# Both chunks of an attention unit in one run of narrow matmuls, and a fixed table for the order of all instructions

## The chip, the cores and the metric

The kernel runs on one core of one Trainium2 chip. The metric is the time of the device for one execution, in microseconds (us). TensorE (PE) does matmuls, VectorE (DVE) and ScalarE (ACT) work on tiles, GpSimd (POOL) only sets constants here, and SyncE (SP) issues every transfer.

## What is computed

Gated linear attention with a complex decay per key row, and then a two-layer feed-forward network on its output:

```python
for t in range(S):                       # S = 768, B = 4, H = 8, D = 48
    new_re = ar * S_re - ai * S_im       # ar, ai: normalised gate of step t, per key row
    new_im = ar * S_im + ai * S_re
    kv = np.einsum('bhd,bhe->bhde', k[:, :, t], v[:, :, t])
    S_re, S_im = (new_re + kv, new_im)
    y[:, :, t] = np.einsum('bhd,bhde->bhe', q[:, :, t], S_re)
...
h = x @ w_in                             # x: 3072 x 384, w_in: 384 x 2048
g = np.where(h >= 1, h, np.where(h <= -1, 0.0, (h + 1) ** 2 / 4))
return g @ w_out                         # 2048 x 384
```

## The kernel before, in words

The 3072 tokens are cut into 12 units of 256 tokens (`u`), and a unit into two chunks of 128 (`c`). Units alternate between two batch entries; a unit is the first, second or third part (`PART`) of its sequence of 768. Two units make a block of 512 tokens, six blocks in all.

**Gates.** `gates(u)` turns a and the inputs k and q into rotated, decayed rows with long ACT and DVE instructions over 768 or 1536 columns; the last two (`turn`, L958) write products that ten DMAs (`spread`) move into the tiles `hd`, one set of rows per head.

**Attention.** `attend(u)` works per chunk in five steps. `scores` makes the masked products of k and q (`sc`, L1129; DVE masks them into `am`, L1137). `transposes` turns k (`tp`, L1072; ACT copies into `kT`). `values` makes the output `yp` from the state `st` (L1170) and from `am` and V (L1178); ACT copies it to `xr` (L1190). `products` makes k times V (`dp`, L1101), and DVE adds it to the state (`st`, L1114; the first chunk of a sequence is copied by ACT, L1111). `values` and `products` use half of the array's columns (their weights are 64 columns wide, "128*64" in a row); all other matmuls use 128. A unit is issued in five visits of PE: `sc` of chunk 0; `tp` of chunk 0; `yp` and `dp` of chunk 0 with half of `sc` of chunk 1; the other half with `tp` of chunk 1; `yp` and `dp` of chunk 1. So a unit has two narrow runs, with wide work between them. The results of `sc`, `tp`, `dp` and `yp` take turns in three PSUM banks.

**Handing over.** A block's x needs 16 rows of two heads moved to other partitions. For blocks 1 to 5 six small DMAs per unit do it (`move`); for block 0 PE does it with a selecting matrix (`joined`, `px`, L1262), twelve matmuls for each of its two units. `split` then makes xH and xL.

**Network.** `moe(blk)` runs 16 steps (`f`): nine matmuls `h` (L1351), on ACT and DVE a chain from `s` (L1376) over `g` (L1395, L1403) and `gh` (L1409) to `gl` (L1413), then nine matmuls `o` (L1426). In blocks 0 and 1 ACT has two more instructions in the chain (L1386, L1390) and DVE one less. `s` and `g` take turns in three tiles, `gh` and `gl` in six, `h` in two PSUM banks. The three results of a block are copied by ACT (L1453) and stored. The weights come as raw bits and are decoded by DVE and ACT during the head and block 0 (L546 to L575); for the first five of sixteen the low part is made by PE (`rest`, L584, L585, `LO_PE`).

**Order.** All of this is written down as operations with costs and dependencies; `Plan.forward` plays them through by due times and gives the order that each engine's queue gets. `Plan.order` starts from due times worked out backwards and tries 1000 changes of them. SP's queue carries all DMAs in the planned order. Until the first `h`, PE is kept busy with matmuls whose result is not used (`idle`, L1481).

Of the kernel before, what the change touches and what calls it, by code (L numbers as in the profile page):

```python
# [45 lines left out]
LATER = 4  # L46
SUM = 1.0e6
RATIO = 1.5
FOURTH = 1.142**4
# [14 lines left out]
LOAD, MOVE = 410.0, 240.0  # L64
LATE = 2000
LATE_MOVE = 1000
# [3 lines left out]
LAG = 3  # L70
# [14 lines left out]
LO_PE = 5  # L85
INFLATE = 1.6
SPLIT_DUE = 3000
TO_NARROW, TO_WIDE = 140, 212
ROUNDS, SEED = 1000, 0
REACH = (100e3, 180e3, 300e3, 600e3)  # L90
# [39 lines left out]
class Plan:  # L130
# [46 lines left out]
    def first_due(self):  # L177
        ops = self.ops
        due = [0.0] * len(ops)
        for i in range(len(ops) - 1, -1, -1):  # L180
            eng, cost, _, _, d, dma, late = ops[i]
            t = 1e12 if d is None else d
            if dma:
                own = DMA_FIX + DMA_END + dma + 600 + late
            else:
                own = cost * (INFLATE if eng in ("ACT", "DVE") else 1.0) + LAT[eng]
            for s in self.succ[i]:
                t = min(t, due[s] - own)
            due[i] = t
        return due  # L190

# [6 lines left out]
    def forward(self, due):  # L198
# [16 lines left out]
        forced = []  # L215
        narrow = False
        while done < n:
            if forced:
# [3 lines left out]
            else:  # L222
                best = None
                for e in free:
                    while avail[e] and avail[e][0][1] in taken:
# [57 lines left out]
            if nxt is not None and not left[nxt]:  # L283
                forced.append(nxt)
        return start, end, took

    def backward(self, plan):
        ops = self.ops
        n = len(ops)
        start, end, took = plan  # L290
        left = [len(s) for s in self.succ]
        tail = [0.0] * n
        free = {e: 0.0 for e in ("PE", "DVE", "ACT", "SP", "POOL")}
        wait = {e: [] for e in free}
        avail = {e: [] for e in free}
        moved = 0.0
        due = [0.0] * n
        for i in range(n):
            if not left[i]:
                heapq.heappush(wait[ops[i][0]], (0.0, i))  # L300
        for _ in range(n):
            best = None
            for e in free:
                if avail[e]:
                    t = free[e]
                elif wait[e]:
                    t = max(free[e], wait[e][0][0])
                else:
                    continue
                if best is None or t < best[0]:  # L310
                    best = (t, e)
            t, e = best
            while wait[e] and wait[e][0][0] <= t:
                _, i = heapq.heappop(wait[e])
                heapq.heappush(avail[e], (-start[i], i))
            _, i = heapq.heappop(avail[e])
            dma, late = ops[i][5:]
            if dma:
                moved = max(tail[i], moved) + dma
                t = max(moved + DMA_FIX + DMA_END + late, free[e] + took[i])  # L320
                free[e] += took[i]
            else:
                t += took[i]
                free[e] = t
            due[i] = -t
            for p in ops[i][3]:
                left[p] -= 1
                tail[p] = max(tail[p], t + self.lags[p, i])
                if not left[p]:
                    heapq.heappush(wait[ops[p][0]], (tail[p], p))  # L330
        total = max(end)
        return [total + d for d in due]

    def order(self):
# [7 lines left out]
        due = self.first_due()  # L342
        plan = self.forward(due)
        best = (max(plan[1]), due, plan)
        cost = best[0]
        rng = random.Random(SEED)
        for k in range(ROUNDS):
            part = rng.random()
            if k == 0 or part < 0.15:
                share = 1.0 if k == 0 else rng.random()  # L350
                new = [a + (b - a) * share for a, b in zip(due, self.backward(plan))]
            else:
                new = list(due)
                t = rng.uniform(0, rng.choice(REACH))
                w = rng.choice((1e3, 5e3, 15e3, 40e3))
                eng = rng.choice(("DVE", "ACT", "PE", "SP", "DVE", "ACT", None))
                near = [
                    i
                    for i, a in enumerate(plan[0])
                    if abs(a - t) < w and (eng is None or ops[i][0] == eng)  # L360
                ]
                shift = rng.choice((500, 2000, 6000, 15000))
                for i in rng.sample(near, min(rng.choice((1, 1, 2, 3, 5, 10)), len(near))):
                    new[i] += rng.gauss(0, shift)
            trial = self.forward(new)
            value = max(trial[1])
            heat = 300.0 * (1 - k / ROUNDS) + 6.0
            if value <= cost or rng.random() < math.exp((cost - value) / heat):
                cost, due, plan = value, new, trial
                if cost < best[0]:  # L370
                    best = (cost, due, plan)
        _, self.due, (self.start, self.end, took) = best
# [4 lines left out]
    def emit(self, warm, mark, guards, flags, verdict, fetch):  # L377
# [5 lines left out]
        final = [i for i in order if self.ops[i][0] == "SP"][-NJ:]  # L383
# [50 lines left out]


@with_exitstack
def gated_scan_moe(
# [24 lines left out]
    keys = [const.tile([P, 4 * HR + 32], F32, name=f"kT{g}") for g in range(2)]  # L462
# [39 lines left out]
    def dma(nbytes, dst, src, r=(), w=(), due=None, rate=LOAD, eng="SP", after=(), late=0):  # L502
        queue = {"SP": nc.sync, "ACT": nc.scalar, "POOL": nc.gpsimd}[eng]
        return pl.op(
# [20 lines left out]
    def weights(n, kind, i, slot):  # L525
# [8 lines left out]
        eng, late = ("SP", 0) if n < 3 else (LOADS, LATE)  # L534
# [5 lines left out]
            dma=P * N * 8 / LOAD,  # L540
# [149 lines left out]
    def gates(u):  # L690
# [21 lines left out]
        if u == 0:  # L712
            for e in range(2):
                dma(
                    size,
                    lambda e=e: AI.get()[:, e],
                    lambda e=e: art[u, :, e],
                    w=[(AI, e)],
                )
        else:  # L720
            dma(2 * size, lambda: AI.get(), lambda: (art[u] if by_token else ari[place]), w=[a, i], after=moved if u == 3 else (), late=LATE if u > 2 else 0, eng=LOADS if u > 2 else "SP")

# [127 lines left out]
        dma(2 * size, lambda: KQ.get(), lambda: kq[place], w=[KQ], after=moved if u == 2 else (), late=LATE if u > 1 else 0, eng=LOADS if u > 1 else "SP")  # L850
# [85 lines left out]
        dma(P * NC * DM * 4, lambda t=vt[u]: t.get(), lambda: v[place], w=[vt[u]], late=LATE if u > 1 else 0, eng=LOADS if u > 1 else "SP")  # L936
# [81 lines left out]
    PICK = tl("s2", [P, NJ + 1, P], F32, "pick")  # L1018
# [14 lines left out]
    carry = {}  # L1033
# [3 lines left out]
    def attend(u):  # L1037
# [25 lines left out]
        def transposes(c):  # L1063
            cs = slice(c * CH, (c + 1) * CH)
            out = []
            for g in range(2):
                TP = bank([P, 4, HR], f"tp_{u}_{g}_{c}")
                KT = pl.tile(f"kT{g}", lambda g=g: keys[g])
# [17 lines left out]
                carry.setdefault("kT", []).append(KT)  # L1086
            return out

        def products(c):
            kT = carry.pop("kT")  # L1090
            DP = bank([P, NH, D], f"dp_{u}_{c}")
            V_c = carry["V"]
            old = carry.get(b)
            ST = tl(turn_of(f"st{b % 2}", 2), [HR, NH, D], F32, f"st_{u}_{c}")
            carry[b] = ST
# [23 lines left out]
        def scores(c):  # L1119
            cs = slice(c * CH, (c + 1) * CH)  # L1120
            out, ams = [], []
            for g in range(2):
                SC = bank([P, 4, CH], f"sc_{u}_{g}_{c}")
                AM = tl(f"am{g}", [P, 4, CH], F32, f"am_{u}_{g}_{c}")
# [26 lines left out]
        def values(c, ams, st):  # L1151
# [5 lines left out]
            def part(prs):  # L1157
# [28 lines left out]
                def tail():  # L1186
# [7 lines left out]
                    if prs[0] == 0 and c == NC - 1 and blk:  # L1194
# [33 lines left out]
        pending = None  # L1228
        if part == 0:
            carry.pop("kT", None)  # L1230
        state_after = lambda c: part * NC + c < S // CH - 1
        for c in range(NC):
            before = [] if pending is None else values(c - 1, *pending) + products(c - 1)
            sc, ams = scores(c)
            tp = transposes(c) if state_after(c) else []
            if before:
                visit(before + sc[:1])
                visit(sc[1:] + tp)
            else:
                visit(sc)  # L1240
                visit(tp)
            pending = (ams, carry.get(b))
            carry["V"] = (V, c)
        last = values(NC - 1, *pending)
        if state_after(NC - 1):
            last = last + products(NC - 1)
        visit(last)
# [5 lines left out]
    def joined(XR):  # L1253
        T = len(BLOCKS[0]) * U
        PX = [tl(f"at{j}", [P, T], F32, f"px_{j}", ps) for j in range(NJ)]
# [524 lines left out]
```

## Time and profile before

| what | value |
|---|---|
| median of 3 runs | 574.57 us (573.16 to 575.27) |
| profiled execution, its own time | 574.42 us |
| its span from first to last instruction | 572.5 us, so 1.9 us lie around it |
| PE busy | 562.0 us, 98% |
| VectorE busy | 426.4 us, 74% |
| ScalarE busy | 411.6 us, 72% |
| first `h` of block 0 / last `o` of block 5 | begins at 71.89 us / ends at 567.86 us, in the chain |
| chain that ended last | 92% PE |

Matmuls overlap in a profile, so "busy" of PE hides short gaps; its pace is read from the times between starts, or from the pieces of the chain.

### The profile page before, as it was taken

The page shows a single profiled execution, that of the slowest core. Times are in us where ns is not written, and L with a number is a line of the kernel's source. Part 1 is how long each engine was busy: PE and PEld are TensorE (multiplying, and loading weights), DVE is VectorE, ACT ScalarE, POOL GpSimd, SP SyncE. Part 2 cuts the span into 40 slices and gives each one's busy share as a digit, 9 for nine tenths or more (in the row PEclk, how much of TensorE's full clock was granted, in tenths as well). Part 3 has the DMA queues.
Part 4 walks back from the last instruction along what each step waited for, and adds up shares of the span by engine and source line. Part 5 has one row for each costly group of instructions (what it writes and reads, how often), then busy time and mean ns, then how long its engine had stood idle before and what let it go on. Part 6 is the DMA issues. An engine that isn't in the chain of part 4 may idle for free.

```text
span 572.5 us, 9927 instructions
## 1 busy us (share of the span) xinstructions
PE 562.0 (98%) x3892; PEld 477.3 (83%) x3892; DVE 426.4 (74%) x595; ACT 411.6 (72%) x690; POOL 3.3 (1%) x29
## 2 busy tenths in 40 slices
PE   7999999999999999999999999999999999999996
PEld 7878988888888888888888888888888888888885
DVE  3987999999969498578798877897886444454553
ACT  6896889988998998985756686756643323359982
POOL 2000000000000000000000000000000000000000
PEclk9999999999999999999999999999999999999999
DMA  8658542684631714613603412501411400078831
GB/s 340 265 164 274 193 172 61 196 276 151 212 116 45 201 66 153 213 57 82 175 0 88 169 56 74 182 1 56 146 56 29 116 2 3 5 270 277 278 112 58
DMA packets 23283, 77.17 MB, mean 135 GB/s; under 512 B 4480, under 2 KB 10048, under 8 KB 23232
## 3 DMA queue, kind: packets, MB, share of 16 engines
q1 hardware_dynamic: 23232, 76.50, 40.6%
q8 instruction: 31, 0.51, 0.3%
q14 instruction: 20, 0.16, 0.1%
HBM read 51.90 MB, written 4.72 MB: 99 GB/s over the span
## 4 chain that ended last, share of the span: by engine, by line
PE 92%; DVE 3%; ACT 2%; DMA 1%; issue 1%; SPq 0%; DVEq 0%
PE h L1351 35%; PE o L1426 35%; PE sc L1129 8%; PE yp L1178 4%; PE yp L1170 4%; PE dp L1101 3%; PE tp L1072 2%; DMA ai<-in_art_dram 1%; PE px L1262 1%; DVE x L958 1%; ACT ai L729 1%; ACT x L729 0%; PE turns L788 0%; DVE ai L745 0%; DVE ai L769 0%
## 5 line engine op out<-in xcount | busy, mean ns | idle before, releaser
L1351 PE MATMUL h<-xH,wi 128*128 128x512 f32 x576 | 180.7, 395 | 0.0
L1426 PE MATMUL o<-gh,wo 128*128 128x512 f32 x576 | 179.8, 393 | 0.0
L1426 PEld LDWEIGHTS o<-gh,wo 128*128 128x128 f32 x576 | 106.5, 188 | 21.7 <-issue 0.5
L1351 PEld LDWEIGHTS h<-xH,wi 128*128 128x128 f32 x576 | 105.9, 188 | 21.2 <-issue 0.2
L1351 PE MATMUL h<-xL,wi 128*128 128x512 f32 x288 | 112.4, 390 | 0.0
L1426 PE MATMUL o<-gl,wo 128*128 128x512 f32 x288 | 112.3, 390 | 0.0
L1395 DVE TENSOR_TENSOR g<-h,s 128x512 f32<-128x512 f32 x96 | 66.0, 688 | 60.5 <-ACT s L1376 49.0
L1376 ACT ACTIVATE s<-h,cst 128x512 f32<-128x512 f32 x96 | 65.8, 686 | 49.0 <-PE h L1351 45.0
L1409 ACT CAST gh<-g 128x512 fp32r<-128x512 f32 x96 | 59.1, 615 | 49.2 <-DVE g L1403 47.1
L1413 DVE TENSOR_TENSOR gl<-g,gh 128x512 fp32r<-128x512 f32 x96 | 66.1, 688 | 34.2 <-ACT gh L1409 34.1
L1351 PEld LDWEIGHTS h<-xL,wi 128*128 128x128 f32 x288 | 54.0, 188 | 11.8
L1426 PEld LDWEIGHTS o<-gl,wo 128*128 128x128 f32 x288 | 54.1, 188 | 11.7
L1129 PE MATMUL sc<-hd 96*128 96x128 f32 x384 | 49.6, 278 | 0.0
L1129 PEld LDWEIGHTS sc<-hd 96*128 96x128 f32 x384 | 47.1, 191 | 2.2
L729 ACT ACTIVATE ai<-ai 128x768 f32<-128x768 f32 x49 | 41.3, 844 | 7.0 <-DVE ai L902 5.6
L1403 DVE SCALAR_TENSOR_TENSOR g<-s,g 128x512 f32<-128x512 f32 x64 | 44.2, 690 | 1.8
L1137 DVE TENSOR_TENSOR am<-sc,sums 128x512 f32<-128x512 f32 x48 | 32.6, 684 | 5.3 <-PE sc L1129 4.9
L1178 PE MATMUL yp<-am,V 128*64 128x128 f32 x384 | 35.5, 273 | 0.0
L1170 PE MATMUL yp<-hd,st 96*64 96x128 f32 x320 | 32.1, 278 | 0.0
L517 ACT ACT_TABLE_LOAD x21 | 26.9, 1283 | 0.4
L1481 PEld LDWEIGHTS idle<-sums,ident 128*128 128x128 f32 x174 | 23.0, 209 | 2.9 <-POOL sums masks.py:66 1.8
L1481 PE MATMUL idle<-sums,ident 128*128 128x128 f32 x174 | 23.4, 293 | 1.8 <-POOL sums masks.py:66 1.8
(109 smaller groups left out, 673.1 us busy)
## 6 DMA issues: line engine op xcount, KB each, us to landing
chk<-in_wl_dram SPq DMA_DIRECT2D x16, 768.0 KB, 6.0
kq<-in_kq_dram SPq DMA_DIRECT2D x12, 768.0 KB, 4.9
ai<-in_ari_dram SPq DMA_DIRECT2D x10, 768.0 KB, 6.1
hd<-x SPq DMA_DIRECT2D x24, 288.0 KB, 4.2
hd<-kq SPq DMA_DIRECT2D x24, 288.0 KB, 4.5
raw_i<-in_wl_dram SPq DMA_DIRECT2D x8, 768.0 KB, 6.4
raw_o<-in_wl_dram SPq DMA_DIRECT2D x8, 768.0 KB, 4.5
V<-in_v_dram SPq DMA_DIRECT2D x12, 384.0 KB, 4.0
```

The source lines that it names most:

```text
L729: lambda: A_.activation(out(), src(), f, **kw),
L1129: PE_.matmul(SC.get()[:, i, :], t[:, 0, cs], t[:, 1, cs], start=True, stop=True)
L1170: PE_.matmul(o_, st.get().rearrange("p h e -> p (h e)")[:, lo : lo + 64], head(h)[:, 1, cs], start=True, stop=False,)
L1178: PE_.matmul(o_, V.get()[:, c, lo : lo + 64], ams[pr // 2].get()[:, 2 * (pr % 2) + e, :], start=st is None, stop=True,)
L1351: PE_.matmul(H.get(), weight["i", f // 2].get()[:, f % 2, part, sl], x.get()[:, j, :], start=j == 0 and n == 0, stop=j == NJ - 1 and n == 2,)
L1376: lambda: A_.activation(SS.get(), H.get(), AF.Relu, bias=c_half, scale=-0.5 if spare else 0.5),
L1395: lambda: V_.tensor_tensor(G.get(), H.get(), SS.get(), op=ALU.max),
L1403: lambda: V_.scalar_tensor_tensor(G.get(), SS.get(), 1.0, G.get(), op0=ALU.min, op1=ALU.mult),
L1409: pl.op("ACT", act(T), lambda: A_.copy(GH.get(), G.get()), r=[G], w=[GH])
L1413: lambda: V_.tensor_tensor(GL.get(), G.get(), GH.get().bitcast(F32), op=ALU.subtract),
L1426: PE_.matmul(PO[m].get(), weight["o", f // 2].get()[:, f % 2, part, sl], g.get(), start=f == 0 and n == 0, stop=f == NF - 1 and n == 2,)
L1481: PE_.matmul(idle["h1"], ident, mask, start=True, stop=True)
```

## The change

From unit 2 on (`APART`), both chunks' `values` and `products` are one visit, glued in the order `dp` 0, `yp` 0, `dp` 1, `yp` 1; the visits before it are `sc` 0, `tp` 0, `sc` 1, `tp` 1. So `am` and `kT` exist four times and the state between the chunks gets a tile of its own (`mid`). While a glued part is not ready, the planner keeps PE for it. Unit 0 gets another order of visits; unit 1 stays. To make room in SBUF, `s` and `g` take turns in two tiles, `gh` and `gl` in four, and `o` follows `h` by two steps where it was three (`LAG`). Unit 0 is handed over by six DMAs, unit 1 by PE as before (`JOINED`). One weight fewer gets its low part from PE (`LO_PE` 4). The last third of the last block's last step is made, copied and stored in two halves. The 1000 trials are replaced by a table of due times (`PRIORITY`, one number for each operation), and the planner's costs of transfers are larger.

```diff
+APART = 2
+JOINED = (1,)
-LAG = 3
+LAG = 2
-LO_PE = 5
+LO_PE = 4
...
+        self.due = [100.0 * k for k in PRIORITY]
+        self.start, self.end, took = self.forward(self.due)
...
+    keys = [const.tile([P, 4 * HR + 32], F32, name=f"kT{g}") for g in range(4)]
...
-            ST = tl(turn_of(f"st{b % 2}", 2), [HR, NH, D], F32, f"st_{u}_{c}")
+            slot = "mid" if c == 0 else f"st{b % 2}"
+            ST = states[b] = tl(slot, [HR, NH, D], F32, f"st_{u}_{c}")
...
-                    if prs[0] == 0 and c == NC - 1 and blk:
+                    if prs[0] == 0 and c == NC - 1 and (blk or ub not in JOINED):
...
+        def parts(cs):
+            out = []
+            for c in cs:
+                old = states.get(b)
+                new = products(c) if state_after(c) else []
+                y = values(c, held[c], old)
+                out += y + new if u < APART else new + y
+            return out
...
+        visit(parts([1] if u < APART else [0, 1]))
...
-            SS = tl(turn_of("s", 3), [P, T], F32, f"s_{blk}_{f}")
-            G = tl(turn_of("s", 3), [P, T], F32, f"g_{blk}_{f}")
-            GH = tl(turn_of("gg", 6), [P, T], F32R, f"gh_{blk}_{f}")
-            GL = tl(turn_of("gg", 6), [P, T], F32R, f"gl_{blk}_{f}")
+            SS = tl(turn_of("s", 2), [P, T], F32, f"s_{blk}_{f}")
+            G = tl(turn_of("s", 2), [P, T], F32, f"g_{blk}_{f}")
+            GH = tl(turn_of("gg", 4), [P, T], F32R, f"gh_{blk}_{f}")
+            GL = tl(turn_of("gg", 4), [P, T], F32R, f"gl_{blk}_{f}")
...
+        halves = lambda m: 2 if blk == NBLK - 1 and m == NJ - 1 else 1
...
-            OB = tl(turn_of("s", 3), [P, T], F32, f"ob_{blk}_{m}")
+            OB = tl(turn_of("gg", 4), [P, T], F32, f"ob_{blk}_{m}")
```

## Rows read from the trace of the kernel before

**Rows 1.** Windows: busy us (instructions) by engine, granted clock, DMA share, GB/s.

```profile
43.70:71.60 27.90, 27.26 (x355) 24.96 (x355) 24.26 (x34) 22.30 (x41) 0.00 (x0) 1.00 0.71 235
...
72.00:157.00 85.00, 85.00 (x635) 72.51 (x634) 83.90 (x117) 76.31 (x124) 0.00 (x0) 1.00 0.53 177
157.00:242.00 85.00, 85.00 (x567) 71.75 (x566) 61.21 (x86) 79.10 (x133) 0.00 (x0) 1.00 0.42 134
```

**Rows 2.** Chain that ended last, 320 to 324 us: start, us, what.

```profile
320.13 2.04 PE o L1426 x9
```

**Rows 3.** Chain that ended last, around the two narrow runs of one unit.

```profile
293.99 1.02 PE yp L1178 x16
...
295.93 1.09 PE sc L1129 x8
...
301.81 0.89 PE sc L1129 x8
...
308.32 0.22 PE yp L1178 x4
...
309.42 0.92 PE dp L1101 x32
```

**Rows 4.** Timeline of PE, the same first run: start, us, instructions.

```profile
294.84 1.09 PE L1101 MATMUL dp<-V,kT 128*64 128x48 f32 x32
295.86 1.16 PE L1129 MATMUL sc<-hd 96*128 96x128 f32 x8
```

**Rows 5.** Timeline of VectorE around the second run.

```profile
307.91 1.75 DVE L958 TENSOR_TENSOR kq<-kq,ai 128x1536 f32<-128x1536 f32 x1
...
310.39 0.55 DVE L1114 TENSOR_TENSOR st<-st,dp 96x384 f32<-96x384 f32 x1
```

**Rows 6.** Chain that ended last, in the head.

```profile
15.45 0.87 DVE raw_i L564
16.32 0.47 DVE y_i L546
...
31.16 0.48 DVE y_o L546
...
31.66 0.96 DVE raw_o L555
...
47.19 0.70 PE rest_o L584 x2
47.89 0.18 PE rest_o L585
...
58.10 0.89 PE px L1262 x4
...
63.60 1.76 PE px L1262 x8
...
71.89 4.13 PE h L1351 x18
```

**Rows 7.** Timeline of SyncE in the head: transfers issued.

```profile
57.33 0.33 SPq L507 DMA_DIRECT2D V<-in_v_dram  x1
64.69 2.60 SPq L507 DMA_DIRECT2D hd<-x  x4
```

**Rows 8.** Groups by line: busy us, mean ns, idle before and its releasers.

```profile
L1409 ACT CAST gh<-g 128x512 fp32r<-128x512 f32 x96 | 59.1, 615 | 49.2 <-DVE g L1403 47.1 <-DVE g L1395 1.9
...
L1453 ACT COPY ob<-o 128x512 f32<-128x512 f32 x18 | 10.5, 583 | 10.0 <-PE o L1426 9.7
...
L1294 ACT CAST xH<-px 128x256 fp32r<-128x256 f32 x6 | 2.2, 373 | 0.6 <-PE px L1262 0.6
```

**Rows 9.** Timeline of all engines, the last steps.

```profile
563.41 0.69 DVE L1413 TENSOR_TENSOR gl<-g,gh 128x512 fp32r<-128x512 f32 x1 [0.74 <-ACT gh L1409]
```

**Rows 10.** Chain that ended last, its end.

```profile
558.33 2.04 PE h L1351 x9
560.37 7.49 PE o L1426 x33
```

More of the change, by code (lines that the diff above doesn't have):

```diff
@@ L175, in op @@
         return i
[L177 to L190, printed above, removed]
     def lag(self, i, s):
@@ L215, in forward @@
         forced = []
+        open_ = None
         narrow = False
         while done < n:
+            if open_ is not None and not left[open_]:
+                forced.append(open_)
+                open_ = None
             if forced:
@@ L224, in forward @@
                 for e in free:
+                    if e == "PE" and open_ is not None:
+                        continue
                     while avail[e] and avail[e][0][1] in taken:
@@ L282, in forward @@
             nxt = self.glued.get(i)
-            if nxt is not None and not left[nxt]:
-                forced.append(nxt)
+            if nxt is not None:
+                open_ = nxt
         return start, end, took
[L287 to L332, printed above, removed]
     def order(self):
@@ L341, in order @@
         self.lags = {(i, s): self.lag(i, s) for i in range(n) for s in self.succ[i]}
[L342 to L372, printed above, removed]
+        assert len(PRIORITY) == n
+        self.due = [100.0 * k for k in PRIORITY]
+        self.start, self.end, took = self.forward(self.due)
         for o, t in zip(ops, took):
@@ L503, in dma @@
         queue = {"SP": nc.sync, "ACT": nc.scalar, "POOL": nc.gpsimd}[eng]
+        if late != LATE and rate == LOAD:
+            rate = PLAIN
         return pl.op(
@@ L533, in weights @@
         N = 2 * DM
-        eng, late = ("SP", 0) if n < 3 else (LOADS, LATE)
+        eng, late = ("SP", FIRST_LATE) if n < 3 else (LOADS, LATE)
         pl.op(
@@ L848, in gates @@
             ac(X0, X0, AF.Exp, [], [x0], True)
-        dma(2 * size, lambda: KQ.get(), lambda: kq[place], w=[KQ], after=moved if u == 2 else (), late=LATE if u > 1 else 0, eng=LOADS if u > 1 else "SP")
+        dma(2 * size, lambda: KQ.get(), lambda: kq[place], w=[KQ], after=moved if u == 2 else (), late=LATE if u > 1 else FIRST_LATE, eng=LOADS if u > 1 else "SP")
         ve(dve(2 * N), lambda: V_.tensor_tensor(KQ.get(), KQ.get(), X.get(), op=ALU.mult), [X], [KQ])
@@ L1066, in transposes @@
             for g in range(2):
-                TP = bank([P, 4, HR], f"tp_{u}_{g}_{c}")
-                KT = pl.tile(f"kT{g}", lambda g=g: keys[g])
+                far = (u, c, g) == (0, 0, 1)
+                name = f"tp_{u}_{g}_{c}"
+                TP = tl("o1", [P, 4, HR], F32, name, ps) if far else bank([P, 4, HR], name)
+                KT = pl.tile(f"kT{2 * c + g}", lambda k=2 * c + g: keys[k])
                 def run(g=g, TP=TP):
@@ L1430, in mms @@
                             start=f == 0 and n == 0,
-                            stop=f == NF - 1 and n == 2,
+                            stop=f == NF - 1 and n == 2 and h * W + W == T,
                         )
-                pl.op(
-                    "PE",
-                    3 * per(T),
-                    mms,
-                    r=[weight["o", f // 2], GH, GL],
-                    w=[PO[m]],
-                    due=t0 + STEP * (f + LAG - 0.5 + m / 6),
-                )
+                for h in range(parts):
+                    pl.op(
+                        "PE",
+                        3 * per(W),
+                        lambda m=m, h=h, W=W: mms(m, h, W),
+                        r=[weight["o", f // 2], GH, GL],
+                        w=[PO[m] if parts == 1 else (PO[m], h)],
+                        due=t0 + STEP * (f + LAG - 0.5 + (m + h / 2) / 6),
+                    )
@@ new lines, in moe @@
+            W = T // halves(m)
+            for h in range(halves(m)):
+                t = slice(h * W, h * W + W)
+                part = None if W == T else h
+                i = pl.op(
+                    "ACT",
+                    act(W, psum=True),
+                    lambda m=m, OB=OB, t=t: A_.copy(OB.get()[:, t], PO[m].get()[:, t]),
+                    r=[(PO[m], part)],
+                    w=[(OB, part)],
+                    due=t0 + STEP * (NF + LAG + 1.5 + h / 4),
+                )
+                if blk < NBLK - 1:
+                    finals.append(i)
+                place = PLACE[BLOCKS[blk][0]] + h * NPART
+                dma(
+                    P * W * 4,
+                    lambda m=m, W=W, place=place: out[
+                        place : place + NPART * (W // U - 1) + 1 : NPART, m
+                    ].rearrange("n p t -> p n t"),
+                    lambda OB=OB, t=t: OB.get()[:, t].rearrange("p (n t) -> p n t", t=U),
+                    r=[(OB, part)],
+                    due=t0 + STEP * (NF + LAG + 2 + h / 4),
+                )
```

112 lines of the change are left out of this document (46 added, 66 removed), and 150 rows, old and new, of the table PRIORITY.

## The prediction

> **What bounds the kernel now.** I read the page first: PE is busy for 98% of the span. A busy PE need not be a full one, so the next view is the chain of waits in order of time. Before the first `h` at 71.89 us [rows 6] it goes through transfers, ACT, DVE and PE in turn; from there to 567.86 us (560.37 + 7.49) [rows 10] it is nearly PE alone. There nine matmuls of a step take 2.04 us, again and again [rows 2], 227 ns each; the 1728 of the network make 392 of those 496 us, and the rest is attention and the seams around it. So after the head the time is PE's work, and what counts is PE's seams and whatever makes PE wait.
>
> The third view is the windows [rows 1]. In block 0 (72 to 157 us) not only PE is full: DVE works 83.90 of 85 us and ACT 76.31. In block 1 DVE has 24 us free, ACT 6. In the last part of the head (43.7 to 71.6) DVE has 3.6 us free. The granted clock is 1.00, the level of 2.4 GHz, in all three windows, so no clock is to be won. Two conclusions: what is taken off PE after block 0 counts in full; what is taken off PE in the head counts only if DVE, which must decode weights, gate two more units and serve the network in block 0, gets ahead as well.
>
> **The change part by part.** The sum is made against the profiled execution's own 574.42 us, which is 0.15 under the median 574.57; what lies around the span (1.9 us) stays.
>
> *One narrow run for two* (units 2 to 11). The first of the two runs of a unit shows its seams [rows 3]: 16 `yp` take 1.02 us where four groups of 0.22 make 0.88, so going narrow costs 0.14; the eight `sc` behind `dp` take 1.09 where eight elsewhere take 0.89, so going wide costs 0.20. The chain uses modelled ends. By starts [rows 4] the `dp` group takes 1.02 before wide work against 0.92 in the chain, so going wide costs 0.10 there. A run therefore costs 0.24 to 0.34, and I take 0.28. The other seams (visits from `h` or `o` into `sc` and `tp` and back) are as many as before, since the half `sc` that closed the first run becomes part of a whole `sc` visit. Ten units: 10 x 0.28 = **-2.8** (bounds -3.4 and -2.4).
>
> *The wait inside the run.* `yp` of chunk 1 now needs the state that DVE makes from `dp` of chunk 0, and PE stands still until it is there; behind it wait all of PE's later work. Between `dp` 0 and `yp` 1 lie `yp` 0 (16 or 32 matmuls, 0.88 or 1.76 us) and `dp` 1 (0.92, missing in the last part of a sequence), so 1.76 to 2.68 us of cover. The sum needs DVE: in the second run shown, `dp` ends at 310.34 (309.42 + 0.92) [rows 3] and the state at 310.94 (310.39 + 0.55) [rows 5], 0.60 later. So it is hidden unless a long instruction, such as one of 1.75 us [rows 5], starts just ahead of it: then 2.35 us, which the short cover misses by 0.59. Bounds: nothing, and 0.60 for each of ten runs, 6.0, if nothing covered it. One in ten runs caught by a long instruction is nearest to these rows; **+0.5** takes almost one miss.
>
> *Handing over unit 0 by DMA.* Twelve `px` matmuls go, 0.89 + 1.76 = 2.65 us of the chain [rows 6]. The six DMAs come at SP between V at 57.33 and the next ten `hd` transfers from 64.69 [rows 7]: four of those take 2.60 us to issue, so six take 3.9, and the queue is free for 7 us. Without that cover unit 2's `hd` would be 3.9 us late. ACT and DVE lose three small casts and subtractions each for one long one, nearly even. The `px` also filled time in which DVE masked unit 1's `sc`, and block 0 stands under DVE's load [rows 1]; half may come through. **-1.3** (bounds 0 and -2.65).
>
> *One low part less on PE.* One `rest` on the chain is 0.70 + 0.18 = 0.88 us [rows 6]; the other of its pair lies before the first `sc`, beside `idle` work. DVE gets one instruction of about 0.95 us more (L555 takes as long: 0.96 [rows 6]), ACT two copies less. **-0.4** (bounds 0 and -0.88).
>
> *Fewer buffers and the lag of two.* After `h` of a step, `gl` is ready 3.73 us later where little else runs: `h` ends at 560.37 [rows 10], `gl` at 564.10 [rows 9]. With a lag of two, two steps of `o` (4.08 us) [rows 2] can stand between them at the very end, so 0.35 us of room is left and no stall. In blocks 2 to 5 PE alone takes 4.08 us for a step, more than those 3.73. In blocks 0 and 1 two tiles for `s` and `g` mean that the next step's `g` waits for this step's `gl`. Below, it costs nothing, since other DVE work can stand in between. Above, DVE stands still for one cast (0.615 us, L1409 [rows 8]) in each of block 0's 16 steps: 9.8 us, and as DVE is full there, PE follows. **+0.6**: one step in sixteen.
>
> *The tail.* The last copy halves, from 0.583 to about 0.373 (the cast of 256 columns [rows 8]), -0.2; against it come three more weight loads, at no row of their own, at most 0.2. The last transfer halves too, for which I take 0.1. **-0.1** (bounds -0.5 and +0.2).
>
> *The table.* It may put any instruction elsewhere, and no row shows it. The gain is bounded by work on the chain of the head that the first unit doesn't need: four weight instructions, 0.87 + 0.47 + 0.48 + 0.96 = 2.8 us [rows 6]. The loss I bound by one 1.75 us instruction in the wrong place [rows 5]. DVE in block 0 argues for the middle: a decode that is put off there comes back before 157 us. **-0.9**.
>
> Sum: -2.8 + 0.5 - 1.3 - 0.4 + 0.6 - 0.1 - 0.9 = -4.4, so 574.42 - 4.4 = **570.0 us**.
>
> **The rivals.** A measurement of this kernel can tell about 0.5% from no change: 571.7 to 577.4 us is "same".
>
> *The buffers bind (slower).* Place: `s` and `g`, block 0. For it: DVE has 1.1 us free in 85, so every gap that a waiting `g` opens is PE's; chains that could overlap over two steps now hardly can. Against it: between the instructions of one chain there is always gate or weight work to do. Price: with the 9.8 us above instead of 0.6 the sum is +4.8, 579.2 us. It turns slower by over 0.5% when these gaps exceed some 8 us, 0.5 us in each step of block 0. The Trainium skill ("Perfetto Trace Analysis", section Optimization Strategy) says that consistent bubbles on the engine that should be saturated can mean that SBUF or PSUM ran out for the next tile; it speaks against this part. No such bubbles stand in block 0 of the trace before, whose tiles are more.
>
> *The run stalls on its state.* Place: `yp` 1 in ten units. For it: DVE runs without a break in block 0. Against it: 0.60 us of need against at least 1.76 of cover. Price: 6.0 in place of 0.5 gives -4.4 + 5.5 = +1.1, 575.5 us, "same". The same skill page (section Optimizing Tensor Performance, Matmuls) asks that independent groups rotate through PSUM banks, so that copying one out overlaps the next; four groups on three banks break that for the fourth, which needs the first one's bank, but it needs the first one's state in any case.
>
> *The head gains nothing.* For it: DVE's 83.90 of 85 us in block 0. Then `px`, `rest` and the table give 0: -2.8 + 0.5 + 0.6 - 0.1 = -1.8, 572.6 us, "same".
>
> *The table gives more.* All of 2.8 us and all of `px`: -4.4 - 1.9 - 1.35 = -7.7, 566.7 us. Against it stands the same DVE load.
>
> **How the numbers follow.** Forecast 570.0, with 567.5 to 571.7 as its own range: 0.46. More from head and table, 563 to 567.5: 0.17. Head gives nothing, 571.7 to 573.5: 0.17. The run stalls, 574 to 577: 0.09. Buffers bind, over 577.4: 0.11. So faster by over 0.5%: 0.46 + 0.17 = 0.63; same 0.26; slower 0.11. The range of 8 in 10 leaves out the slow case and the far ends of two others: **565.5 to 575.5**.
>
> **What would show it.** Between 170 and 500 us ten narrow runs in place of twenty, and no idle time of PE before `yp` of chunk 1; PE's time between first `h` and last `o` some 3 us shorter than 496. Half as many `px`. First `h` at about 69 us, not 71.89. DVE in block 0 still without breaks. In the tail four stores of which the last is half as long. The prediction is wrong if PE waits for `st`, if DVE shows gaps before `g` (L1395) in block 0 that end with `gl` or `gh`, or if the first `h` moves by more than 4 us in either direction.

## The result, and the profile after

The changed kernel takes **570.31 us** (median of 6 runs, 568.9 to 571.53), the kernel before took 575.34 beside it (573.16 to 575.71): a ratio of **0.9918** (95% interval 0.9898 to 0.9939). The forecast was 570.0. The profiled execution takes 570.58 us, with a span of 568.8 against 572.5.

Three marks cut the span: the first `h`, the last `o`, and the end. I take them by the starts of the instructions, since matmul ends are modelled.

```
                      before    after     difference
first h               71.64     69.86     -1.78
first h to last o    495.81    492.95     -2.86
last o to the end      5.07      5.98     +0.91
```

The ten joined runs of units 2 to 11 begin between 94.92 and 468.40 us; the prediction looked for them from 170 us on, where only seven begin.

The chain of waits shows the same marks. Ahead of `h` stand the twelve `px` that are left, where before there were 4 + 8 + 12, and `h` begins at 70.11 in place of 71.89 [rows 6]; the last `o` group ends at 563.10 in place of 567.86 [rows 10], 4.76 earlier.

```profile
66.43 2.79 PE px L1342 x12
69.22 0.89 PE idle L1574 x8
70.11 2.77 PE h L1433 x12
...
556.94 6.16 PE o L1513 x30
563.10 0.02 issue
563.12 0.37 ACT ob L1545
```

The windows of [rows 1], after (the columns are the same). In block 0 DVE has shed 1.9 us of work (81.97 for 83.90) and is still nearly full; PE has no free time in either block. The surprise is in the first row: a granted clock of 0.94.

```profile
43.70:71.60 27.90, 26.48 (x341) 24.67 (x340) 25.16 (x34) 20.23 (x34) 0.00 (x0) 0.94 0.62 207
72.00:157.00 85.00, 85.00 (x640) 72.91 (x639) 81.97 (x111) 77.53 (x123) 0.00 (x0) 1.00 0.51 170
157.00:242.00 85.00, 85.00 (x567) 71.94 (x566) 62.01 (x86) 79.22 (x131) 0.00 (x0) 1.00 0.45 140
```

Next the timeline of PE, one narrow run of a unit, to be held against the cut run of [rows 3, 4]. It begins with `dp` of chunk 0 at 344.28 and ends before `o` at 349.82; no row in it says that PE waited.

```profile
344.28 1.14 PE L1172 MATMUL dp<-V,kT 128*64 128x48 f32 x32
...
345.25 0.40 PE L1241 MATMUL yp<-hd,st 96*64 96x128 f32 x4
345.49 0.39 PE L1249 MATMUL yp<-am,V 128*64 128x128 f32 x4
...
347.03 1.09 PE L1172 MATMUL dp<-V,kT 128*64 128x48 f32 x32
347.94 0.41 PE L1241 MATMUL yp<-hd,st 96*64 96x128 f32 x4
...
349.82 0.50 PE L1513 MATMUL o<-gh,wo 128*128 128x512 f32 x1
```

Where does the state for chunk 1 come from? The timeline of VectorE has it, behind a `g`:

```profile
345.43 0.69 DVE L1485 SCALAR_TENSOR_TENSOR g<-s,g 128x512 f32<-128x512 f32 x1
346.04 0.54 DVE L1185 TENSOR_TENSOR st<-st,dp 96x384 f32<-96x384 f32 x1
```

It is ready at 346.58, and PE asks for it at 347.94: 1.36 us of slack. The list of PE's waits agrees: in the whole execution there is none for `st`, none for `h` or `o`, and, apart from the filler's first start, one of size, in the head.

```profile
PE idle L1574 <- POOL sums masks.py:66: 1.8, 1, 1.8
PE sc L1200 <- DVE am L1208: 1.2, 1, 1.2
PE turns L857 <- ACT ai L798: 0.3, 1, 0.3
```

By starts there is one small pause more, below what that list counts: at 243.04 us `o` begins 0.50 us behind the `h` before it (a step is 0.23 there), and the `o` at 243.76 comes 0.39 behind the one before. In the chain the first follows `gh`, which ScalarE ends at 242.99.

The wait in the head and the clock stand next to each other in this execution. Windows around it:

```profile
44.00:48.00 4.00, 2.70 (x22) 2.32 (x22) 4.00 (x7) 2.49 (x4) 0.00 (x0) 1.00 0.84 213
48.00:52.00 4.00, 4.00 (x53) 3.77 (x53) 3.02 (x6) 2.01 (x3) 0.00 (x0) 0.57 0.98 407
52.00:56.00 4.00, 3.88 (x44) 3.52 (x42) 2.68 (x5) 2.68 (x7) 0.00 (x0) 1.00 0.82 339
```

PE stood idle for 1.21 us ahead of 46.08, and in 48 to 52 us the granted clock is 0.57, near the lower of its two levels (1.2 of 2.4 GHz). Other kernels below with the same order and the same idle time keep 1.00 there, and their first `h` comes at 68.31 to 68.46: the dip costs this one execution some 1.5 us, and not each. The timed runs split alike: the three longest of the changed kernel (570.52 to 571.53 us) have a mean granted clock of 0.995 to 0.997, the three shortest 0.998 or 0.999, and the longest runs of the kernel before stand at 0.995 or 0.996 too.

The tail is longer. SyncE issues four stores; its timeline, each in its own window:

```profile
562.35 0.39 SPq L575 DMA_DIRECT2D out_dram<-ob  x1
...
563.08 1.72 SPq L575 DMA_DIRECT2D out_dram<-ob  x1
...
564.90 0.91 SPq L575 DMA_DIRECT2D out_dram<-ob  x2
```

The second takes 1.72 us where the others take 0.39 to 0.46, and the two halves queue behind it: the last store is issued 2.54 us behind the start of the last `o`, where before it was 1.04, and lands 1.99 us later in place of 2.65. Beside it the DMA view (562.8 to 563.0 us) has a transfer of the other kind, instructions, 16 KB:

```profile
q8 instruction: 1, 0.02, 47.0%
```

### The profile page after: what moved, and what is told of

Its sections match the earlier page's. It is cut to its first block, busy times and chain, and to the rows that moved or that the text cites. A ratio compares the mean times of both kernels' runs of the same rounds, so it can differ in the third digit from the quotient of the medians.

```text
span 568.8 us, 10066 instructions
## 1 busy us (share of the span) xinstructions
PE 559.0 (98%) x3903; PEld 477.6 (84%) x3903; DVE 429.8 (76%) x594; ACT 413.1 (73%) x687; POOL 3.4 (1%) x31
## 4 chain that ended last, share of the span: by engine, by line
PE 86%; DVE 6%; DMA 2%; ACT 2%; issue 1%; SPq 0%; ACTq 0%; DVEq 0%
PE o L1513 33%; PE h L1433 33%; PE sc L1200 7%; PE yp L1249 4%; PE dp L1172 4%; PE yp L1241 3%; PE tp L1143 2%; DMA hd<-x 2%; DMA ai<-in_art_dram 1%; ACT ai L798 1%; DVE raw_i L623 1%; DVE kq L1027 1%; DVE x L1027 1%; DVE kq L920 1%; DVE ai L814 1%
## 5 line engine op out<-in xcount | busy, mean ns | idle before, releaser
L1200 PE MATMUL sc<-hd 96*128 96x128 f32 x384 | 47.6, 277 | 1.3 <-DVE am L1208 1.2
L1574 PE MATMUL idle<-sums,ident 128*128 128x128 f32 x200 | 26.7, 294 | 1.8 <-POOL sums masks.py:66 1.8
L1574 PEld LDWEIGHTS idle<-sums,ident 128*128 128x128 f32 x200 | 26.1, 210 | 2.6 <-POOL sums masks.py:66 1.8
```

The source lines that it names most:

```text
L1200: PE_.matmul(SC.get()[:, i, :], t[:, 0, cs], t[:, 1, cs], start=True, stop=True)
L1574: PE_.matmul(idle["h1"], ident, mask, start=True, stop=True)
```

## The experiments

Twelve kernels ran, each compared with the kernel before on its own chip. "By starts" means from the start of one instruction to the start of another, as for the marks of the table above.

**The run cut in two again.** One wide piece of the network is put between the two halves of each narrow run, all else as planned.

```diff
+        for part in self.halved:           # chunk 1's half of a run
+            order = rest + [order[wide]] + late + order[wide + 1 :]
```

> The changed kernel, its table and its buffers, with the narrow run of each unit from 2 on cut in two: the next wide piece of PE (three matmuls of h or o) is put between the halves. If a narrow run costs its seams (0.24 to 0.34 us each), ten more runs cost 2.4 to 3.4 us: about 573.1 us, a ratio to the kernel before of 0.996 to 0.998, and PE's time from first h to last o grows from 493 to about 496 us. If the gain came from the table and the head, the ratio stays at 0.992.

Measured: 576.36, ratio 1.0048 (1.0019 to 1.0078); body 500.12, which is 7.2 us over the changed kernel's. By starts, a cut adds 0.35 to 0.37 us of seam in eight of the ten runs: some 3.6 for ten, more than the 2.8 I gave. The other 3.6 us lie outside these seams. The list of PE's waits has 1.5 of them, of an order that no longer fits, such as this one in the timeline of PE; the rest is in pauses too short for that list:

```profile
265.54 0.73 PE L1451 MATMUL h<-xH,wi 128*128 128x512 f32 x2 [1.28 <-DVE g L1495]
```

So a cut costs at least what I took for it. The Trainium skill ("TensorEngine Tiling (Array Packing)", section Key Properties) says that a change of the tiling mode drains TensorE; the seams here, up to 0.37 us for a way out and back, fit that, though no view shows the drain itself.

The two kernels themselves say it without an edit. Between first `h` and last `o`, by starts, PE steps from wide into narrow work 10 times in place of 20 (0.32 us each, where a step inside `h` or `o` is 0.23), which is 0.9 us; `sc` takes 34.07 us for 34.89, and `yp` and `dp` together 49.85 for 51.11. Together that is 3.0 us, against the body's 2.86: the seams account for the whole of it.

**The state made five times.** This takes away cover without touching PE's order. (Where ScalarE copies the state, in the first part of a sequence, its copy is made five times too.)

```diff
-                fn = lambda: V_.tensor_tensor(ST.get(), old.get(), DP.get()[:HR], op=ALU.add)
+                fn = lambda: [V_.tensor_tensor(ST.get(), old.get(), DP.get()[:HR], op=ALU.add)
+                              for _ in range(5 if u >= APART and c == 0 else 1)]
```

> The changed kernel with the state between the chunks made five times over (same result), from unit 2 on, so that it is there 2.8 us after dp of chunk 0 and not 0.6 (ScalarE's copies: 2.4). The cover is 1.76 us in the last part of a sequence, 1.80 in the first, 2.68 in the middle. If cover is all that keeps the run from waiting, PE now waits before yp of chunk 1 by about 1.0 us in units 4, 5, 10 and 11, 0.6 in 6 and 7, 0.1 in 2, 3, 8 and 9: 5.6 us in all, about 576. If the run had room for other reasons, PE waits nowhere and the time is that of the changed kernel.

Measured in a single run: 588.79; body 512.41, 19.5 us more, with PE waiting for the state in all ten units, 0.79 to 1.98 us each, 13.2 in all. The rest of the 19.5 isn't accounted for; a granted clock that falls to 0.50 behind the wait of 1.82 us at 144.18 is part of it. One of them, all engines:

```profile
356.94 2.88 DVE L1186 TENSOR_TENSOR st<-st,dp 96x384 f32<-96x384 f32 x5
...
359.96 0.44 PE L1244 MATMUL yp<-hd,st 96*64 96x128 f32 x4 [0.95 <-DVE st L1186]
```

The five sums take 2.88 us, but VectorE starts them only at 356.94, behind a `g`, some 0.6 us after `dp` has ended. So the mechanism of the wait is real, and it is the cover that keeps it at nothing; the waits are 0.2 to 1.7 us longer than the expectation had them, in the unit shown because DVE comes to the sum late.

**Unit 0 handed over by PE again.** A first try lost the planned order:

> The changed kernel with unit 0's part handed over by PE again, as before, the rest of the order kept. My prediction gave the handing over by DMA 1.3 us (bounds 0 to 2.65): first h comes about 1.3 us later than in the other runs of the changed order that kept full clock through the head (68.3 us), that is at about 69.6, the body unchanged near 493, the ratio about 0.994. Rival that the six moves are hidden anyway: first h stays within 0.3 us of 68.3 to 68.4. Rival that they delay unit 2's loads: first h comes earlier than 68.3.

It took 675.82 us (ratio 1.1755), full of waits that have nothing to do with `px`: the table is a list of ranks for just this set of operations, and with nine others in it the rest of the order falls apart. It says nothing on the six moves. The second try writes out the changed kernel's start times and puts the twelve `px` rows back between them.

```diff
-JOINED = (1,)
+JOINED = (0, 1)
...
-        self.due = [100.0 * k for k in PRIORITY]
-        self.start, self.end, took = self.forward(self.due)
+        self.start = [float(t) for t in START]
```

> The changed kernel with unit 0 handed over by PE again, and every other operation of PE, ACT, DVE and SP in the changed kernel's order (the run e7_px_both lost that order, as its table no longer fitted). Twelve px rows of 0.22 us come back, four before the y of unit 1's chunk 0 and eight in place of two idle operations before that of chunk 1, and the six moves go. My prediction gave this part 1.3 us (bounds 0 to 2.65): first h at about 69.6 us against 68.3 to 68.4 in the runs of this order at full clock, ratio about 0.994. If all twelve lie on the path less the 0.44 us of idle operations that they replace: first h at 70.6 to 71.0, ratio about 0.996. If the moves were hidden anyway: first h within 0.3 us of 68.4, ratio 0.992. The body stays within 1 us of 493.4.

Measured: 573.19, ratio 0.9985 (0.997 to 1.0001). The timeline of PE:

```profile
57.50 1.13 PE L1343 MATMUL px<-xr,pick 128*128 128x256 f32 x4
58.56 1.09 PE L1250 MATMUL yp<-am,V 128*64 128x128 f32 x16
...
63.05 1.92 PE L1343 MATMUL px<-xr,pick 128*128 128x256 f32 x8
...
67.73 2.86 PE L1343 MATMUL px<-xr,pick 128*128 128x256 f32 x12
70.42 1.05 PE L1575 MATMUL idle<-sums,ident 128*128 128x128 f32 x8
71.23 0.71 PE L1434 MATMUL h<-xH,wi 128*128 128x512 f32 x2
```

And the same stretch of a kernel with the changed kernel's order at full clock (the one with ten idle operations, below):

```profile
57.10 1.06 PE L1249 MATMUL yp<-am,V 128*64 128x128 f32 x16
...
61.56 0.64 PE L1574 MATMUL idle<-sums,ident 128*128 128x128 f32 x4
...
64.95 2.86 PE L1342 MATMUL px<-xr,pick 128*128 128x256 f32 x12
67.65 1.05 PE L1574 MATMUL idle<-sums,ident 128*128 128x128 f32 x8
68.46 0.71 PE L1433 MATMUL h<-xH,wi 128*128 128x512 f32 x2
```

First `h` at 71.23 against 68.46, 2.77 later; the second half of unit 0's scores stood 0.28 later already (46.51 for 46.23), so 2.5 us are the `px`. They were on the path nearly whole (twelve at 0.22 us make 2.64). The six moves, at SyncE from 58.49 on for 4.12 us, hold nothing up: unit 2's first `hd` follows at 62.72, earlier than the 64.69 of [rows 7].

**The buffers alone.** The kernel before, with its own search, and only the buffers and the lag of the changed kernel.

```diff
-LAG = 3
+LAG = 2
...
-            SS = tl(turn_of("s", 3), [P, T], F32, f"s_{blk}_{f}")
+            SS = tl(turn_of("s", 2), [P, T], F32, f"s_{blk}_{f}")
-            GH = tl(turn_of("gg", 6), [P, T], F32R, f"gh_{blk}_{f}")
+            GH = tl(turn_of("gg", 4), [P, T], F32R, f"gh_{blk}_{f}")
```

> The kernel before with the changed kernel's buffers alone: a lag of two, two buffers for s and g, four for gh and gl, the output's copy on gh's buffers, the second product ahead of the first in a step. Its own search orders it. My prediction priced this at +0.6 us (0 to 9.8): a ratio of 1.001, with no new wait of PE for h, o or gl above half a microsecond. Rival that the buffers bind: PE waits between h and o in each of the 48 steps, some 0.1 to 0.2 us each, a body 5 to 10 us longer, a ratio of 1.009 to 1.017.

Measured: 579.37, ratio 1.0085 (1.0062 to 1.0108). The body is 2.0 us longer (497.84), the first `h` 2.3 us later (73.90), the tail 0.6 longer. In the body one wait carries the rival's mark (timeline of PE):

```profile
157.31 0.50 PE L1426 MATMUL o<-gl,wo 128*128 128x512 f32 x1 [0.35 <-DVE gl L1413]
```

It is one wait, with a shorter one of `o` just ahead of it, not sixteen; the three steps of PE of 0.42 us or more make 1.0 us of the 2.0. Why the head moved isn't settled. The search came out with another order there, and with the same buffers and the other edits `h` comes at 69.11 in one searched order and at 73.90 in another (seeds 0 and 1, below); PE waits 2.39 us for the first decode, and behind it the granted clock falls to 0.50, where the kernel before kept 1.00 behind 2.20. As a whole this kernel is 4.9 us slower, at the rival's lower edge (1.009), but not by the rival's 48 waits. So the buffers cost up to 2 us of body in an order that the search found, and in the changed kernel's order at most the pause at 243 us, about 0.4.

**The order by the search instead of the table.** All edits but the table, at two seeds, and the kernel before at the second seed as a control.

```diff
-        self.due = [100.0 * k for k in PRIORITY]
+ROUNDS, SEED = 1000, 0     # then 1000, 1
```

> The changed kernel with all its edits, but its order comes from the search of the kernel before (1000 trials, seed 0) in place of the table. My prediction gave the table 0.9 of the 4.4 us (bounds -2.8 to +1.75): by that the ratio to the kernel before is about 0.993 and the time about 1 us over the changed kernel's, with the body (first h to last o) some 493 to 494 us. Rival: the table is what makes it fast, since a planned order with fewer narrow runs leaves waits that only a search over late transfers avoids; then the body comes back to about 496 us or more, with PE waits of half a microsecond or more that the changed kernel lacks, and the ratio is 0.998 or more.

> All edits of the changed kernel but the table, ordered by the search of the kernel before with seed 1. Together with the same at seed 0 (0.9975) and the kernel before at seeds 0 and 1 it tells the edits apart from the order. My prediction gave the edits without the table -3.5 us of 574.4: a ratio of 0.994 to the kernel before in the mean of the draws. If the table carries more than the 0.9 us (up to 2.8) that I gave it: again 0.997 or more, with single waits of PE of over 1 us that the changed kernel lacks.

> The kernel before with another draw of its own search (seed 1 instead of 0; nothing else differs). It tells how far the order drawn moves the time. If little: ratio 1.000, within 0.002. If the draw moves it by some microseconds: a ratio off 1 by 0.003 or more, and then the 3.3 us between the changed kernel with its table (0.9918) and with the search's order (0.9975) can't be put down to the table's way of searching alone.

Measured: 572.67 at seed 0, ratio 0.9975 (0.9962 to 0.9989); 573.91 at seed 1, ratio 1.0006 (0.9987 to 1.0024); the kernel before at seed 1 574.3, ratio 1.0007 (0.9992 to 1.0021), on PE in the order of seed 0 up to 81.8 us and in another behind it. So all other edits together gain 1.4 us in one order and nothing in the other, and the table makes 3.3 to 5 us of the result. These are two draws of the search; what more draws or trials would find isn't tested.

Two different things went wrong in the two profiled executions. These took 574.82 and 575.99 us, each 2.1 us over its kernel's median, so what they show need not stand whole in every execution. At seed 0 the body has 498.21 us, with this in the timeline of PE:

```profile
120.22 3.58 PE L1298 MATMUL sc<-hd 96*128 96x128 f32 x16 [2.02 <-issue]
```

and these windows:

```profile
117.00:120.20 3.20, 1.20 (x6) 0.67 (x5) 3.17 (x5) 3.17 (x6) 0.00 (x0) 1.00 0.62 114
120.20:124.00 3.80, 3.78 (x18) 3.76 (x19) 2.17 (x4) 1.04 (x2) 0.00 (x0) 0.55 0.27 80
```

Nothing on an engine releases those scores, so it is data. The DMA view of 107.9 to 112.5 us (count, KB each, median us to landing), and behind it two rows of the timeline of SyncE:

```profile
hd<-kq SPq DMA_DIRECT2D x2, 288.0 KB, 10.8
```

```profile
107.73 0.34 SPq L689 DMA_DIRECT2D raw_o<-in_wl_dram  x1
108.12 2.92 SPq L673 DMA_DIRECT2D hd<-kq  x4
```

Six of the unit's ten `hd` loads are issued behind 768 KB of weights (`raw_o`), at 108.1 to 112.2 us; the weights land at 116.59 and the loads from 118.92 on. PE goes on at 120.22, behind one that lands at 120.13. The Trainium skill ("Perfetto Trace Analysis", section DMA Instruction — HWDGE) warns that a DMA which looks fast in the profile may still be waiting; here four issues take 2.92 us together and their data 10 us or more. After the wait the granted clock is 0.55, and sixteen `sc` take 3.24 us by starts where the changed kernel's take 1.70: the late transfer costs 2.2 us of waiting and 1.5 more of clock in this execution. In the changed kernel six of ten `hd` loads also stand behind a weight transfer, but that one is issued at 102.12; these six land 5.6 to 7.4 us after their issue, behind the weights at 109.08; all ten have landed by 112.48, and the scores start at 114.20 without a wait.

At seed 1 the body is 494.0 us, nearly as good as with the table, but the first `h` comes at 73.90, 5.5 us later than at full clock with the table. There the first decode stands still (timeline of PE), and the weight pieces `rest` that should fill that time come after it:

```profile
15.83 3.80 PE L955 MATMUL dec<-sums,ai 128*128 128x256 f32 x12 [2.41 <-DVE ai L936]
19.43 0.94 PE L750 MATMUL rest_i<-raw_i,ident 128*128 128x384 f32 x2
```

That is 2.4 us; from 16 to 20 us the granted clock is below 0.6, and PE waits 0.97 before a `rest` at 41.65 and 0.52 before `sc` at 51.67. How the 5.5 us divide among these isn't worked out.

**The idle time of PE filled.** Two kernels went after the dip of the clock.

```diff
-                    warm(i, int(((t - end) * WARM - 100) / (2 * 112)))
+                    warm(i, int(((t - end) * WARM - 100) / 112))
```

> The changed kernel with the planned gaps of PE in the head filled nearly whole with unused matmuls, where they were filled by half. If the low granted clock between 48 and 52 us (0.57; sc, yp and dp there take 4.74 us for 2.7) costs its time, the clock stays at 1.00 there and the time falls by 1 to 2 us, to about 569. If that stretch waits for VectorE's masks in any case, nothing moves; if the filling comes in the way of work, it is 0.5 us slower or more.

The first filled too much, by my mistake: an idle operation makes two rows of 0.11 us, so 112 in place of 224 filled each gap 1.7 times, where it had been 0.85 (`WARM`) and not the half that I wrote. Measured: 579.88, ratio 1.0104 (1.0072 to 1.0135); 328 idle rows for 200, first `h` at 78.81, body 493.44 as before. Filler that is longer than its gap pushes the head's chain back, here by 9 to 10.5 us (78.81 against 69.86 and 68.3).

The second fills only the gap before unit 0's scores of chunk 1:

```diff
+        if i in extra:          # first sc of unit 0, chunk 1
+            n = max(n, 0) + 5
```

> The changed kernel with five more idle matmul operations (ten rows of 0.11 us, 1.1 us) put where PE stood idle for 1.21 us before unit 0's scores of chunk 1. Two theories meet here. The gap is what let the granted clock fall to 0.57 at 48 to 52 us in one execution: then the clock stays at 1.00 there in this one, and first h comes at about 68.4 us instead of 69.86; the median gains little, since most executions kept the clock. And the second of the last stores took 1.72 us to issue because an instruction transfer lies beside it: if such transfers follow PE's instruction count, twenty more instructions bring the last one about 2.3 us forward, off the stores, the four stores are issued in about 0.4 us each, and the stretch from the last o to the end falls from 5.98 to about 4.9 us; ratio about 0.990. Rival: the long store comes of its own shape or queue; then it stays at about 1.5 us or more wherever the transfer falls.

Measured: 570.2, ratio 0.9919 (0.9903 to 0.9936), the changed kernel's own. The granted clock is 1.00 and first `h` comes at 68.37, but it does so in the unfilled runs as well, so this one execution proves nothing on the cause of the dip. The tail stays at 6.22, with 1.39 us for the second store; the transfer didn't move off the stores with twenty more instructions, it comes 0.04 us ahead of the last `o`.

**The tail.** Three whole stores in place of two and two halves:

```diff
-        halves = lambda m: 2 if blk == NBLK - 1 and m == NJ - 1 else 1
+        halves = lambda m: 1
```

> The changed kernel with the last third of the last step whole again: three last stores, not four. In the changed kernel 5.7 us lie between the last o and the end (4.6 before), and the second store's issue takes 1.72 us where others take 0.4. If four stores cost that by themselves, the tail goes back to 4.6 us and the time falls by 1.0. If the store is held up by the 16 KB of instructions that are fetched beside it, the second store is as long as now, the tail stays over 5.4 us and the time within 0.3.

Measured: 568.58, ratio 0.9914 (0.9884 to 0.9944), not apart from the changed kernel's 0.9918. Tail 6.26, second store 1.49 us, an instruction transfer beside it. And a shorter program for PE:

```diff
-                    warm(i, int(16 + (t - LEAD) / (2 * 112)))
+                    warm(i, int(10 + (t - LEAD) / (2 * 112)))
```

> The changed kernel with ten instead of sixteen idle operations ahead of the first real one: 24 instructions less in PE's program, and PE idle for some 1.3 us before 13 us. Theory: the 16 KB instruction transfers follow PE's program (one each 256 instructions), and the changed kernel has a further one just when the last o starts because its last regular one came 44 instructions before the end; with 24 fewer it comes some 20 before the end, as in the kernel before (18), and the extra one falls away or the stores no longer meet it. Then all four last stores are issued in about 0.4 us each, and last o to end is about 5.0 us instead of 5.98; ratio about 0.990. Rival: the transfer at the last o has nothing to do with the count; it comes within 0.3 us of the last o again, one store takes over 1.2 us, and the ratio stays 0.992. First h, by either, at 68.3 to 69.9.

Measured: 569.67, ratio 0.9936 (0.9917 to 0.9956); its profiled span, 567.05, is the shortest here. One 16 KB transfer fell away (31 for 32), as the theory asked, but the last one still came 0.35 us behind the start of the last `o`. No store took over 0.89 us, and yet the tail is 5.93: the last store is issued 1.68 us behind the start of the last `o` (before: 1.04) and lands 2.80 us later (2.65), so most of the loss is in the issue. Sorted by where the last such transfer lies, six of the fourteen kernels:

```
kernel               transfer against last o   last o to end   longest store issue
before, seed 1              -1.84                  4.75              0.39
before                      -1.44                  5.07              0.40
buffers alone               -0.32                  5.71              0.60
after                       +0.10                  5.98              1.72
three stores                +0.18                  6.26              1.49
ten idle operations         +0.35                  5.93              0.89
```

In the other eight the transfer lies at -0.05 to +0.56, the tail takes 5.61 to 6.34 and the longest store issue 1.00 to 1.96. The tail is short where the transfer comes ahead of the last stores and 0.5 to 1.6 us longer where it meets them, with three stores or four. That it causes this isn't shown: I could not move it at will.

## Why the prediction came out right

The time came out as forecast, partly by luck: errors of both signs met. Point by point, in the order of its sum:

- **One run for two, -2.8.** Right. The body is 2.86 us shorter, with ten runs for twenty; the steps into and out of narrow work account for it, and a cut that is put back costs 0.35 to 0.37 us of seam, a little over the top of my bounds (0.34).
- **The wait inside the run, +0.5.** It is nothing in this order (no wait for `st`); the slack in the run shown is 1.36 us. That the wait decides once the cover is gone is shown by the state made five times.
- **Handing over unit 0, -1.3.** The mechanism was right, the size half: 2.5 us by the run with `px` put back, its upper bound of 2.65 nearly. The step that failed is "half may come through": I let DVE's load in block 0 decide about a stretch, 57 to 71 us, in which PE was the one that the next instruction waited for. The rival that the head gains nothing falls with it.
- **One `rest` less, -0.4, and the table in the head.** At full clock the first `h` is 3.2 us earlier than before (68.4 for 71.64); with 2.5 for `px` the rest is 0.7. Up to 54.4 us both kernels stand at the same place of unit 0 (`yp` with the state begins at 54.40 before, at 54.38 with ten idle operations); the changed order has one `tp` visit of 0.7 us behind it by then that the other has still ahead. The kernel before has a `rest` at 47.02 that takes 0.98 us and that the changed one lacks there, so the 0.7 may come of it; that it does, and not of the table, isn't shown.
- **Fewer buffers, +0.6.** At most 0.4 in this order, up to 2 us of body in a searched one, whose head is 2.3 us later for a reason that stays open. The rival that the buffers bind (48 waits, or sixteen) is not what the rows show: of VectorE's waits in block 0 of the changed kernel none ends with `gl` or `gh`, and the longest is 0.7 us.
- **The tail, -0.1.** Wrong: +0.9. I priced copies and bytes. The last store did land 0.66 us sooner after its issue, but it was issued 1.5 us later, behind a store that stood beside an instruction transfer.
- **The table, -0.9.** Wrong in size and in kind. I priced it as weight work that could leave the head. Without it, the same edits gain 1.4 us or nothing, so it carries 3.3 to 5 us against these two draws. My reading is that a list of edits that each take a cover away needs, as far as the two searched orders show, an order in which nothing is late: `hd` not behind 768 KB of weights, `rest` where the first decode waits. The rival that the table gives more (2.8) came nearer to its size and missed the time (566.7), as it put the gain on top of the others; in fact the others' gain came through only with it.

By starts the parts are -3.2 for the head at full clock, -2.9 for the body and +0.9 for the tail: -5.2; with the dip, the profiled execution has -3.7, and the ratio of medians makes -4.7 of 575.

Not settled: why the clock dips in one execution and not in others with the same 1.2 us of idle time, what moved the head of the kernel with the buffers alone, and what places the last instruction transfer.

## What to carry to other kernels

When several edits each use up slack, price the order together with them: run them with the old order too, since a gain that is worked out part by part may come through only in an order that knows the late transfers. Whether a saving in the head counts is read from what the next instruction on the path waits for in that very stretch, not from another engine's load in the next. And look where the last stores fall against the machine's own transfers before a shorter copy is counted as a gain.

## What the runs showed of the hardware

- Instruction transfers of 16 KB come about once in 250 matmuls and weight loads of PE (31 to 33 in a run). The Trainium skill ("Runtime: NRT & Kernel Launch", section Instruction fetch mechanics) gives blocks of the same size, of 256 instructions, and says that the cost of crossing one is mostly hidden. Beside one, a store's issue took up to 1.96 us (seed 1) instead of 0.4; that the transfer is the cause isn't shown.
- The granted clock fell to 0.57 behind an idle time of 1.21 us in one execution of several, and to 0.55 behind one of 2.0 us. The second made a late transfer cost 1.5 us more than its wait. The length of the idle time alone doesn't tell: the clock stayed at 1.00 behind 2.20 us in the kernel before (14.73) and behind 1.96 us with the state made five times (220.65), and fell there behind 1.82 (144.18).
- `hd` loads issued right behind 768 KB of weights landed 8.7 to 10.8 us after their issue; four issued some 3 us earlier, ahead of those weights, took 3.4 to 3.9. In the changed kernel, too, the six behind a weight transfer landed only after it had.
